# A gated recurrence with a cosine-gated two-layer block on one core: the second group's second layer as seven half-block products, and a read-back moved behind the first turned keys

## The chip, the cores and the metric

The kernel runs on one core of one Trainium2 chip. The core has a matrix engine (TensorE, PE in the profile, with its weight loads shown as PEld), a vector engine (VectorE, DVE), a scalar engine (ScalarE, ACT), GpSimd (POOL) and a queue engine (SyncE, SP) that issues most of the DMA transfers. ACT and POOL issue some transfers too (ACTq, POOLq). The metric is the device time of one run in microseconds, and the measure of a kernel is the median of its runs.

## The reference

There are 4 batches, 8 heads, 768 steps and 48 channels per head. The first part is a recurrence with a complex gate, and the second part is a layer pair on its output.

```python
mag = sqrt(a_re*a_re + a_im*a_im);  scale = minimum(mag, 0.999) / (mag + 1e-6)
for t in range(768):                       # per batch and head; S is 48 x 48, complex
    S = (a_re + i*a_im)[t] * scale[t] * S + outer(k[t], v[t])      # k, v are real
    y[t] = q[t] @ real(S)
x = y as (3072 tokens, 384)
h = x @ w_in                               # 384 x 2048
out = (h * cos(h)) @ w_out                 # 2048 x 384
```

## The kernel before, in words

The 768 steps of a batch are cut into chunks of 128, which gives 24 chunks in all. Two chunks make a group, so there are 12 groups, numbered from 0. Groups 0 and 1 are written out by hand, with their order on each engine fixed by the order of the text. From group 2 on, a loop over `n` places closures on a line from 0 to 1 with a function `weave`: each list of steps has a stretch of that line, and the steps are called in order of their places. A scheduling layer then gives each engine its own order. Every engine works through its own order, and a row that waits holds up all rows behind it on that engine.

One group passes through these steps, whose tile names are those of the profile:

- **Powers.** `log_steps` makes the logarithm of the gate (`lg`, `mag`, `rs`, `tan`), `p_powers` sums it over the steps of a chunk on PE (`lgs`) and makes `P` and `Q` by two exponentials each, `even_steps` rounds them, and `row_out` and `row_back` write the last row of `P` to memory (`row`) and read it back turned (`end`). `p_end` then scales `end`, which `state_next` needs. From group 2 on, `lg` and the angle are split into a high and a low part (`hi`, `lo`) before PE sums them (`lgs`, `phs`).
- **Keys.** `p_apply`, `g_phase` and `g_trig` make `ks` and `qs`, the queries and keys with the gates' powers and angles in them. Groups 0 and 1 turn them on PE (`turn`, tile `tp`) and ACT copies them out (`kT`, `qT`). From group 2 on, DVE transposes blocks (`tr`) and three transfers bring them into place (`moved`, `kT`, `qT`).
- **Chunk.** `f_scores` multiplies queries and keys (`sc`) and DVE masks them (`atm`); `state_sums` and `state_next` carry the state (`sp`, `state`); `f_out` makes the output (`yp`), ACT copies it (`yT`), and two transfers, one behind the other, turn it into the layers' input (`x<-yT`, then `xT<-x`).
- **First layer.** `mm1` multiplies (`hp`, 48 products of 128 x 256 per group), ACT takes the cosine (`gate`) and a sum of squares for a range check (`junk`), and DVE multiplies (`gate<-hp,gate`). There are eight `gate` tiles of 128 x 512, each with two blocks of 128 channels for the group's 256 tokens.
- **Second layer.** Groups 0 and 1 use `mm2`: for each of the two chunks, 16 products of 128 x 384 into one tile `op`, four at a time, which ACT then copies out. Groups 2 to 11 use seven products of half blocks, as in Strassen's method: `mixed` makes sums and differences of the gate's half blocks on DVE (four rows of 128 x 256 for each of four values of `p`, tiles `s` and `gate<-gate`), `quarters` and `last_quarter` make those of `w_out` once for all groups (12 rows `t_s`, `t_a` of 128 x 384 and 4 rows `w_out<-w_out`), and `seventh` runs one product: 8 matmuls of 128 x 192 in two parts of four. Products 0, 3, 5 and 6 add up in one tile (`sum`), the other three go to `op`.

The constant that decides is `PLAIN = 2`: groups below it use `mm2`. PE runs one 32-bit matmul of the text as two rows, so 16 matmuls show as 32 rows. Many rows carry the line of a helper: L687 is `matmul`, and L676 and L707 are the helpers through which all DVE rows and most ACT rows pass, so the tile names tell the steps apart.

Four places of the text matter for the change. In group 0, after the angles, the text has

```python
    row_back(0, 0, G, scalar)
    busy(10)
    g_stack(0, 0, 1)
    ...
    turn(0, 0)
    lows(0, 1)
    piece(0)
    f_scores(0, 0)
```

`row_back` with `scalar` issues its two transfers from ACT's queue, `busy` is idle work for PE, `lows` is an ACT step of the conversion of `w_in` and `w_out` from 64-bit numbers, and `piece` is a DVE step of it. The other three places are the load of group 1 (`load(1, ("re", "im", "k", "q", "v"))`, on SP), the text around group 1's first half of `mm2` (`upper = second(1, 0)`), and the `weave` of `n = 2`, in which group 1's second layer, group 2's chunks and group 3's powers lie side by side.

Of the kernel before, what the change touches and what calls it, by code (L numbers as in the profile page):

```python
# [11 lines left out]
F32 = mybir.dt.float32  # L12
# [7 lines left out]
ALU = mybir.AluOpType  # L20
# [467 lines left out]
def fast_path(ctx, tc, q, k, v, a_re, a_im, moe_w_in, moe_w_out, out, least, odd, wide,  # L488
# [7 lines left out]
    nc = tc.nc  # L496
    B, H, S, D = q.shape
    DM, DF = moe_w_in.shape
    C = 128
    NCH = S // C  # L500
    G = 2
    N = B * NCH
    NG = N // G
# [5 lines left out]
    NJ = DF // C  # L509
# [13 lines left out]
    pm = ctx.enter_context(tc.tile_pool(name="pm", bufs=3, space=PSUM))  # L523
# [10 lines left out]
    late = {}  # L534
# [8 lines left out]
    def behind(ins, other):  # L543
        tc.add_manual_dep(ins.ins, other.ins.name, mybir.DependencyInfo(
            mybir.DependencyClass.NoSync, mybir.DependencyReason.DATA))
# [15 lines left out]
    Y = [dict() for _ in range(N)]  # L561
# [5 lines left out]
    def load(g, names, i=None, put=nc.sync.dma_start):  # L567
        for name in names:
            ap = {"re": a_re, "im": a_im, "q": q, "k": k, "v": v}[name]
            if name not in X[g]:  # L570
                X[g][name] = ld.tile([C, G, H, D], F32, tag=name, name=name,
                                     bufs=2 if name == "v" else 1)
            b, c = divmod(g * G + (i or 0), NCH)
            one, n = i or 0, G if i is None else 1
            steps = ap[b].rearrange("h (c p) d -> p c h d", p=C)[:, ds(c, n)]
            tile_ = X[g][name][:, ds(one, n)]
            parts = [(0, C, 0)]
            if name in ("re", "im") and g >= PEG:

                parts = [(0, C - 16, 1), (C - 16, C - 1, 1)]  # L580
                put(out=tile_[C - 1:C], in_=steps[0:1])
            for i_ in range(n):
                for lo, hi, by in parts:
                    put(out=tile_[lo:hi, i_], in_=steps[lo + by:hi + by, i_])  # L584
# [99 lines left out]
    vector, scalar = Ordered(nc.vector, "vector"), Ordered(nc.scalar, "scalar")  # L684

    def matmul(out, **kw):
        chain(nc.tensor.matmul(out, **kw), "tensor")  # L687
# [27 lines left out]
    def spans(g):  # L715

        return [(i, 1) for i in range(G)] if g == 0 else [(0, G)]
# [120 lines left out]
    def row_back(g, i, n, queue):  # L838
        row = X[g]["row"][ds(i * DM, n * DM)]
        end = X[g]["end"][:, ds(i * H, n * H)]  # L840
        for a in range(2):
            queue.dma_start(out=end[ds(a * D, D)], in_=row.rearrange("(x d) -> d x", d=D))

    def p_even(g, i, n):
        for _ in even_steps(g, i, n):
            pass
# [254 lines left out]

    def mm2(g, i, j0, nj):
        if j0 == 0:
            Y[g * G + i]["op"] = pm.tile([C, DM], F32, tag="acc" if g == i else "m", name="op",
                                         bufs=1 if g == i else 2)
        ps = Y[g * G + i]["op"]
        for j in range(j0, j0 + nj):
            matmul(ps, lhsT=X[g]["gate"][j // 2][:, j % 2, ts(i, C)], rhs=w_out[:, j],
                   start=(j == 0), stop=(j == NJ - 1))
        if j0 + nj == NJ:  # L1110
            ot = msb.tile([C, DM], F32, tag="ot", name="ot")
            scalar.mul(out=ot, in_=ps, mul=1.0 / (in_scale * out_scale))
            nc.sync.dma_start(out=out[ts(g * G + i, C), :], in_=ot)
# [1 line left out]

    PLAIN, HJ, E2 = 2, NJ // 2, DM // 2
    b11, b12, b21, b22 = (w_out[:, ds(r * HJ, HJ), ds(c * E2, E2)]
                          for r in range(2) for c in range(2))  # L1120
    right = {"a11": b11, "a12": b21, "s3": b12, "s4": b22}
# [1 line left out]
    def quarters():  # L1123

        for name in "s1", "s2", "a22":
            right[name] = stage["pool"].tile([C, HJ, E2], F32, name="t_" + name)
        t1, t2, t4 = (right[name] for name in ("s1", "s2", "a22"))
        for j in range(0, HJ, 2):
            for t, a, b in (t1, b12, b11), (t2, b22, t1), (t4, b21, t2):
                vector.tensor_tensor(out=t[:, ds(j, 2)], in0=a[:, ds(j, 2)],  # L1130
                                     in1=b[:, ds(j, 2)], op=ALU.subtract)

    def last_quarter():

        for j in range(0, HJ, 2):
            yield lambda j=j: vector.tensor_tensor(
                out=b12[:, ds(j, 2)], in0=b22[:, ds(j, 2)], in1=b12[:, ds(j, 2)],
                op=ALU.subtract)
# [64 lines left out]
    def products(g, lo, hi):  # L1203
        if g < PLAIN:
            return []
        return [lambda p=p, part=part: seventh(g, p, part)
                for p in (0, 1, 3, 2, 5, 4, 6)[lo:hi] for part in range(2)]

    def mixes(g, lo, hi):
        return [lambda p=p: mixed(g, p) for p in range(lo, hi)] if g >= PLAIN else []  # L1210

    def weave(*parts):

        items = []
        for p, (part, lo, hi) in enumerate(parts):
            part = list(part)
            items += [(lo + (hi - lo) * (i + 0.5) / len(part), p, t)
                      for i, t in enumerate(part)]
        for _, _, t in sorted(items, key=lambda x: x[:2]):
            t()  # L1220
# [4 lines left out]
    def keys(g):  # L1225

        if not 0 <= g < NG:
            return
        for i, n in spans(g):
            yield lambda i=i, n=n: g_trig(g, i, n)  # L1230
            yield lambda i=i, n=n: (g_stack(g, i, n), p_end(g, i, n))
            for name in "kT", "qT":
                if g >= PEG:
                    yield lambda i=i, n=n, name=name: f_transpose(g, i, n, name)
# [4 lines left out]
    def powers(g):  # L1239
        return [lambda i=i: p_powers(g, i) for i in range(G)]  # L1240

    def prods(g):
        if not 0 <= g < NG:
            return
        if g not in (1, 2):
            yield from powers(g)
            yield lambda: g_angle(g, 0, G)
        yield lambda: (g_carry(g), g_split(g))
        yield lambda: (p_even(g, 0, G), p_apply(g, 0, G))

    def logs(g):
        yield from each(g_log, g)
        if 0 <= g and g + 1 < NG:
            yield lambda: load(g + 1, ("re", "im"))

    def phases(g):
        return [lambda i=i: g_phase(g, i) for i in range(G)] if 0 <= g < NG else []

    def chunks(g):
        for n in range(g * G, g * G + G):  # L1260
            for hh in range(2):
                yield lambda n=n, hh=hh: f_scores(n, hh)
            yield lambda n=n: f_state(n)
            yield lambda n=n: f_out(n)
        yield lambda: (f_x(g), f_xt(g))
        if g + 2 < NG:
            yield lambda: load(g + 2, ("k", "q", "v"))

    def first(g):
        order = range(NJ // 2) if g < PLAIN else (0, 4, 1, 5, 2, 6, 3, 7)  # L1270
        return [lambda jp=jp: mm1(g, jp) for jp in order]

    def second(g, i):
        return [lambda j0=j0: mm2(g, i, j0, 4) for j0 in range(0, NJ, 4)] if g < PLAIN else []

    def wait_for(tile):

        chain(nc.gpsimd.tensor_copy(out=after, in_=tile), "gpsimd")
# [14 lines left out]
    turns = [constant(sums_np[0] * np.float32(1.0 / math.pi), "turns", pool=stage["pool"])]  # L1293
    last = constant(last_np, "last", pool=stage["pool"])
    ident = constant(np.eye(C, dtype=np.float32), "ident", pool=stage["pool"])
    load(1, ("re", "im", "k", "q", "v"))
    ones = constant(sums_np[1], "sums_turned", nc.sync, stage["pool"])
    exact = consts.tile([C, C], F32R, name="exact")
    alls = consts.tile([C, C], F32R, name="alls")
# [26 lines left out]
    p_apply(0, 0, 1)  # L1326
    g_phase(0, 1)
    g_trig(0, 1, 1)
    row_back(0, 0, G, scalar)
    busy(10)  # L1330
    g_stack(0, 0, 1)
    p_apply(0, 1, 1)
# [12 lines left out]
    def lows(*ks):  # L1345
        for k in ks:
            pieces[k][1]()
# [14 lines left out]
    def turn(g, i):  # L1362
        for name in "kT", "qT":
            for hh in range(2):
                f_turn(g, i, name, hh)

    turn(0, 0)
    lows(0, 1)
    piece(0)
    f_scores(0, 0)  # L1370
# [180 lines left out]
    piece(15)  # L1551
    X[3]["steps"] = log_steps(3, 0, G)
    next(X[3]["steps"])
    upper = second(1, 0)
    for t in upper[:2]:
        t()
    sums(1, 6, 8)
    pair(12, 2)
# [3 lines left out]
        mm1_gate(1, jp)  # L1562
    room.close()
    stage.update(pool=ctx.enter_context(tc.tile_pool(name="late", bufs=1)), bufs=1)
    quarters()
    for n in range(2, NG):
        weave((mixes(n - 1, 2, 4), 0.0, 0.12), (logs(n + 1), 0.0, 0.02), (chunks(n), 0.0, 0.36),
              (upper[2:] if n == 2 else [], 0.0, 0.2), (products(n - 1, 0, 2 + (n < NG - 1)), 0.0, 0.36),
              (prods(n + 1), 0.25, 0.27), (second(n - 1, 1), 0.36, 0.5),
              (products(n - 1, 2 + (n < NG - 1), 7), 0.4, 0.56),  # L1570
              (phases(n + 1), *((0.472, 0.476) if n == PLAIN else (0.516, 0.524))),
              (keys(n + 1), *((0.5, 0.62) if n == PLAIN else (0.53, 0.64))),
              (last_quarter() if n == PLAIN else [], 0.9, 1.0), (first(n), 0.56, 1.0),
              (mixes(n, 0, 2), 0.9, 1.0), (guarded(n - 1, per) if n > 3 else [], 0.1, 0.9))
    checked = verdict(late)

# [96 lines left out]
```

## Time and profile before

| | |
|---|---|
| median of 3 runs | 657.82 us (657.73 to 659.49) |
| the profiled execution | 657.8 us, of which the profile spans 656.0 us |
| granted clock of TensorE, mean | 0.998 |
| PE busy | 641.3 us, 98% of the span, 4075 rows |
| PEld busy | 575.7 us, 88% |
| DVE busy | 492.4 us, 75%, 799 rows |
| ACT busy | 392.5 us, 60%, 726 rows |
| chain that ended last | PE 86%, DMA 6%, SP's queue 2%, DVE 2%, ACT 2% |

A row of the timeline has its start in the span, its duration (of all merged rows where it ends in xN), the engine, the line, the operation, the tiles as written from read, the shapes, and in square brackets how long the engine stood idle before it and what ended that. The duration of a row runs to its end; where rows of an engine follow each other without a wait, the distance from start to start is shorter than that, since they overlap.

### The profile page before, as it was taken

What the parts mean: (1) busy time and instruction counts of PE and PEld (TensorE: products, weight loads), DVE (VectorE), ACT (ScalarE), POOL (GpSimd) and SP (SyncE); (2) the same over time, 40 slices, a digit from 0 to 9 for tenths busy, and PEclk for the clock granted to TensorE, in tenths of its full rate; (3) what the DMA queues carried; (4) which work ended last, traced back from release to release, by engine and by line L of the source; (5) the groups of instructions that cost most, each with busy time, mean ns of one, the idle gap of its engine ahead of it and who ended that gap; (6) DMA issues with size and microseconds to landing.
All of it is one profiled execution on the core that took longest, in us unless ns stands there. A gap on an engine that the chain in (4) does not pass through costs nothing.

```text
span 656.0 us, 10759 instructions
## 1 busy us (share of the span) xinstructions
PE 641.3 (98%) x4075; PEld 575.7 (88%) x4075; DVE 492.4 (75%) x799; ACT 392.5 (60%) x726; POOL 32.0 (5%) x53
## 2 busy tenths in 40 slices
PE   8899999999999999999999999999999999999996
PEld 5688867777999899899899899899899999999996
DVE  6899989878687688786787777876877878862251
ACT  7788687293583594494585485485476476433330
POOL 4010100000000010010010010000000000000000
PEclk9999999999999999999999999999999999999999
DMA  9969664727626757737838736836936853364001
GB/s 239 224 187 219 196 189 102 190 60 181 145 49 151 186 135 157 193 98 167 217 78 182 206 92 160 207 95 133 245 104 133 224 127 94 112 135 119 25 1 31
DMA packets 232920, 94.90 MB, mean 145 GB/s; under 512 B 208701, under 2 KB 221246, under 8 KB 232858
## 3 DMA queue, kind: packets, MB, share of 16 engines
q1 hardware_dynamic: 225320, 68.51, 45.9%
q0 software_dynamic: 5824, 25.50, 11.9%
q8 instruction: 34, 0.56, 0.4%
q10 hardware_dynamic: 1714, 0.11, 0.2%
q14 instruction: 28, 0.23, 0.1%
HBM read 69.28 MB, written 24.81 MB: 143 GB/s over the span
## 4 chain that ended last, share of the span: by engine, by line
PE 86%; DMA 6%; SPq 2%; DVE 2%; ACT 2%; issue 1%; ACTq 0%; DVEq 0%
PE hp L687 34%; PE op L687 16%; PE sum L687 15%; PE sc L687 6%; PE yp L687 6%; PE sp L687 4%; DMA v<-in_v_dram 2%; PE phs L687 2%; SPq L584 1%; DMA xT<-x 1%; PE lgs L687 1%; DMA qT<-moved 1%; DMA x<-yT 1%; PE yr L687 1%; SPq L936 1%
## 5 line engine op out<-in xcount | busy, mean ns | idle before, releaser
L687 PE MATMUL hp<-xT,w_in 128*128 128x256 f32 (+1 forms) x1176 | 252.7, 376 | 1.0 <-DMA xT<-x 1.0
L687 PEld LDWEIGHTS hp<-xT,w_in 128*128 128x128 f32 x1176 | 219.9, 190 | 31.5 <-DMA xT<-x 0.9
L707 ACT ACTIVATE gate<-hp,half_pi_b 128x512 f32<-128x512 f32 x96 | 66.0, 687 | 120.2 <-PE hp L687 120.2
L676 DVE TENSOR_TENSOR gate<-hp,gate 128x512 f32<-128x512 f32 x96 | 65.7, 685 | 47.2 <-ACT junk L676 47.1
L687 PE MATMUL op<-w_out,gate 128*128 128x192 f32 (+1 forms) x448 | 100.7, 375 | 0.0
L687 PEld LDWEIGHTS op<-w_out,gate 128*128 128x128 f32 x448 | 76.0, 190 | 16.8 <-issue 2.0
L676 ACT ACTIVATE junk<-hp 128x512 bf16<-128x512 f32 x96 | 56.6, 590 | 0.0
L687 PE MATMUL sum<-t_s,s 128*128 128x192 f32 x320 | 56.3, 329 | 0.0
L687 PEld LDWEIGHTS sum<-t_s,s 128*128 128x128 f32 x320 | 52.1, 190 | 1.5 <-issue 1.5
L676 DVE TENSOR_TENSOR atm<-sc,causal 128x512 f32<-128x512 f32 x48 | 32.9, 688 | 25.7 <-PE sc L687 25.6
L687 PEld LDWEIGHTS sc<-qT,kT 96*128 96x128 f32 x384 | 47.2, 192 | 5.4 <-ACT qT L676 2.5
L687 PE MATMUL sc<-qT,kT 96*128 96x128 f32 x384 | 49.2, 277 | 2.5 <-ACT qT L676 2.3
L676 ACT ACTIVATE ot<-sum 128x192 f32<-128x192 f32 x40 | 12.8, 322 | 52.8 <-PE sum L687 52.6
L676 DVE SCALAR_TENSOR_TENSOR ot<-op,ot 128x192 f32<-128x192 f32 x41 | 13.6, 353 | 39.5 <-PE op L687 37.9
L687 PE MATMUL yp<-atm,v 128*48 128x128 f32 x352 | 33.6, 277 | 0.9 <-ACT Q L707 0.6
L703 ACT ACT_TABLE_LOAD x24 | 30.8, 1283 | 1.1 <-PEq L1657 0.7
L687 PE MATMUL yp<-qT,state 96*48 96x128 f32 x304 | 29.7, 272 | 0.0
L687 PE MATMUL sum<-w_out,gate 128*128 128x192 f32 x160 | 29.7, 330 | 0.0
L687 PE MATMUL sp<-v,ks 128*96 128x48 f32 x320 | 29.7, 246 | 0.0
L687 PEld LDWEIGHTS sp<-v,ks 128*96 128x96 f32 x320 | 29.6, 165 | 0.0
L676 ACT COPY yT<-yp 48x512 f32<-48x512 f32 x44 | 25.2, 573 | 7.4 <-PE yp L687 6.9
L676 ACT CAST tan<-phs 128x384 int32<-128x384 f32 x24 | 11.4, 482 | 29.4 <-PE phs L687 29.4
(145 smaller groups left out, 985.7 us busy)
## 6 DMA issues: line engine op xcount, KB each, us to landing
moved<-tr SPq DMA_DIRECT2D x20, 768.0 KB
raw<-in_moe_w_in_dram POOLq DMA_DIRECT2D x16, 768.0 KB, 5.3
raw<-in_moe_w_out_dram POOLq DMA_DIRECT2D x16, 768.0 KB, 4.9
kT<-moved SPq DMA_DIRECT2D x40, 192.0 KB
qT<-moved SPq DMA_DIRECT2D x10, 768.0 KB
k<-in_k_dram SPq DMA_DIRECT2D x24, 192.0 KB
q<-in_q_dram SPq DMA_DIRECT2D x24, 192.0 KB
v<-in_v_dram SPq DMA_DIRECT2D x24, 192.0 KB
```

What stands on the lines that cost most here:

```text
L584: put(out=tile_[lo:hi, i_], in_=steps[lo + by:hi + by, i_])
L676: ins = getattr(self.engine, op)(**kw)
L687: chain(nc.tensor.matmul(out, **kw), "tensor")
L703: chain(nc.scalar.preload_act_table_set(table))
L707: chain(nc.scalar.activation(func=func, **kw))
L936: nc.sync.dma_start(out=X[g][name][:, ds(i * H, n * H), q4], in_=moved[q4])
```

## The change

Group 1 joins the groups whose second layer is seven products (`PLAIN = 1`). Its first product is placed where the first half of `mm2` stood, and the others in the `weave` of `n = 2`. With it, all sixteen DVE rows of group 1's `mixed` come into that stage; `quarters` becomes a list of steps that is woven in there, and `last_quarter` moves from the end of that stage to its front. `mm2`, now used by group 0 alone, takes both its tiles from the two buffers "m" and none from "acc", which `sum` needs. In the start, `row_back` of group 0 moves behind `turn(0, 0)`, and the load of group 1's values `v` moves behind the loads of its gates, keys and queries. The scheduling layer had issued those two `v` loads right behind group 0's.

```diff
     def mm2(g, i, j0, nj):
         if j0 == 0:
-            Y[g * G + i]["op"] = pm.tile([C, DM], F32, tag="acc" if g == i else "m", name="op",
-                                         bufs=1 if g == i else 2)
+            Y[g * G + i]["op"] = pm.tile([C, DM], F32, tag="m", name="op", bufs=2)
...
-    PLAIN, HJ, E2 = 2, NJ // 2, DM // 2
+    PLAIN, HJ, E2 = 1, NJ // 2, DM // 2
...
         for j in range(0, HJ, 2):
             for t, a, b in (t1, b12, b11), (t2, b22, t1), (t4, b21, t2):
-                vector.tensor_tensor(out=t[:, ds(j, 2)], in0=a[:, ds(j, 2)],
-                                     in1=b[:, ds(j, 2)], op=ALU.subtract)
+                yield lambda t=t, a=a, b=b, j=j: vector.tensor_tensor(
+                    out=t[:, ds(j, 2)], in0=a[:, ds(j, 2)], in1=b[:, ds(j, 2)], op=ALU.subtract)
...
-    def second(g, i):
-        return [lambda j0=j0: mm2(g, i, j0, 4) for j0 in range(0, NJ, 4)] if g < PLAIN else []
...
-    load(1, ("re", "im", "k", "q", "v"))
+    load(1, ("re", "im", "k", "q"), put=lambda **kw: late.update(load=nc.sync.dma_start(**kw)))
+    load(1, ("v",), put=lambda **kw: behind(nc.sync.dma_start(**kw), late["load"]))
...
     g_trig(0, 1, 1)
-    row_back(0, 0, G, scalar)
     busy(10)
...
     turn(0, 0)
+    row_back(0, 0, G, scalar)
     lows(0, 1)
...
-    upper = second(1, 0)
-    for t in upper[:2]:
+    for t in products(1, 0, 1):
         t()
...
-    quarters()
     for n in range(2, NG):
-        weave((mixes(n - 1, 2, 4), 0.0, 0.12), (logs(n + 1), 0.0, 0.02), (chunks(n), 0.0, 0.36),
-              (upper[2:] if n == 2 else [], 0.0, 0.2), (products(n - 1, 0, 2 + (n < NG - 1)), 0.0, 0.36),
-              (prods(n + 1), 0.25, 0.27), (second(n - 1, 1), 0.36, 0.5),
-              (products(n - 1, 2 + (n < NG - 1), 7), 0.4, 0.56),
-              (phases(n + 1), *((0.472, 0.476) if n == PLAIN else (0.516, 0.524))),
-              (keys(n + 1), *((0.5, 0.62) if n == PLAIN else (0.53, 0.64))),
-              (last_quarter() if n == PLAIN else [], 0.9, 1.0), (first(n), 0.56, 1.0),
+        early, cut_ = n == 2, 2 + (n < NG - 1)
+        weave((mixes(n - 1, 0 if early else 2, 4), 0.0, 0.24 if early else 0.12),
+              (logs(n + 1), 0.0, 0.02), (chunks(n), 0.0, 0.36),
+              (quarters() if early else [], 0.01, 0.2), (last_quarter() if early else [], 0.3, 0.36),
+              (products(n - 1, int(early), cut_), 0.12 * early, 0.36),
+              (prods(n + 1), 0.25, 0.27), (products(n - 1, cut_, 7), 0.4, 0.56),
+              (phases(n + 1), 0.516, 0.524), (keys(n + 1), 0.53, 0.64), (first(n), 0.56, 1.0),
               (mixes(n, 0, 2), 0.9, 1.0), (guarded(n - 1, per) if n > 3 else [], 0.1, 0.9))
```

## The prediction

> **What bounds the kernel now.** The page first: PE is busy 98% of the span and carries 86% of the chain that ended last, so a microsecond that reaches PE's order in the middle reaches the end. But a share over the whole span does not say who sets the pace in the two stretches that the change touches, so I read their timelines. The start, first ACT's queue, then who waited:
>
> ```profile
> 22.93 1.02 ACTq L676 DMA_DIRECT2D end<-row  x2
> 24.00 1.07 ACT L676 COPY kT<-tp 96x512 f32<-96x512 f32 x2 [3.01 <-DMA v<-in_v_dram]
> 25.60 2.05 PE L687 MATMUL sc<-qT,kT 96*128 96x128 f32 x16 [2.28 <-ACT qT L676]
> 26.80 0.69 DVE L676 TENSOR_TENSOR atm<-sc,causal 128x512 f32<-128x512 f32 x1 [1.33 <-PE sc L687]
> ...
> 30.04 0.86 ACT L749 ACTIVATE lg<-re 128x768 f32<-128x768 f32 x1
> 31.67 0.96 DVE L676 TENSOR_TENSOR lg<-lg,tan 128x768 f32<-128x768 f32 x1
> 33.75 0.16 DVE L676 TENSOR_SCALAR end<-end 96x16 f32<-96x16 f32 x1
> ```
>
> ACT stands 3.01 us before it can copy keys that PE had turned from 21.30 on: its two `end` issues wait for older transfers, and the chain names the last `v` load (10.88, 12.75 us in flight). PE loses 2.28 us and DVE 1.33 us to that.
>
> From here to 122 us DVE is the engine without slack: the view of waits for that stretch has six entries, 3.7 us in 100. The middle, group 2's stage:
>
> ```profile
> 121.59 1.02 DVE L676 TENSOR_TENSOR t_s<-w_out 128x384 f32<-128x384 f32 x2
> ...
> 129.52 0.69 DVE L676 TENSOR_TENSOR atm<-sc,causal 128x512 f32<-128x512 f32 x1 [2.23 <-PE sc L687]
> ...
> 146.69 0.95 DVE L676 SCALAR_TENSOR_TENSOR lg<-mag,lg 128x768 f32<-128x768 f32 x1
> 147.71 0.24 SPq L835 DMA_DIRECT2D row<-lg  x1
> 148.04 1.51 SPq L1048 DMA_DIRECT2D x<-yT  x2
> 149.30 1.96 DVE L676 TENSOR_TENSOR w_out<-w_out 128x384 f32<-128x384 f32 x4
> ...
> 156.39 7.82 PE L687 MATMUL hp<-xT,w_in 128*128 128x256 f32 x35 [0.33 <-DMA xT<-x]
> ```
>
> Between 121.59 and 146.69 DVE idles in six places, 5.8 us in all (2.23, 0.46, 0.84, 0.62, 1.04, 0.62). The SP queue sends `row` when DVE's last `lg` is done and only then the `x` transfers behind it; `hp` of group 2 starts 8.35 us after the `x` issue. So two orders end in that `hp`: PE's products and DVE's way to `lg`.
>
> **Part 1, the start.** The move takes the `end` issues out from ahead of four copies. PE's `tp` rows start at 21.30 and 22.24, the first half of the keys is done at about 21.92. ACT is free from 20.98, so four copies (spacing 0.48) run from 21.95 to 23.95, against 24.00 to 26.04. `sc` starts at 23.5 and not at 25.60, and DVE's first mask follows its row of 24.91 without a wait. The two issues then stand on ACT between the last copy and the two `raw` rows of `lows`; they cost 0.34 + 0.31 us of issue if nothing holds them. `raw` ends near 26.6 (27.82 before), the next copies start 1.5 earlier (28.13 had waited 0.31 for PE), and `lg<-re` comes at 28.5. DVE's own order, with 1.33 and 0.20 of waiting gone, would bring 31.67 to 30.1; ACT allows the same. Gain: 1.5 us, and as DVE stays full until 122 us it is kept. No trace row shows what holds the moved issues: they now wait for `row` and for group 1's first `im` load, which takes the queue place of the `v` load that landed by 22.93. Bounds: 2.1 (ACT's whole shift) to 0. Holding `v` moves two loads of 192 KB on SP's queue behind `q`; group 1 uses them at 66 us, and its gates come forward. Nothing else waits for them, and I cost it at nothing.
>
> **Part 2, PE's products.** `mm2` of group 1 is 2 x 16 products in 64 rows of 384 columns; the chain has 16 such rows in 5.16 us, 0.3225 each, 20.64 us. Seven products are 56, 112 rows of 192; the chain has 16 in 2.60, 0.1625 each, 18.20. PE has 2.44 us less to do.
>
> One rule speaks against it. The Trainium skill, "TensorE: Matmul & The Clock Gate", section "Back-to-back issue gap", gives a sustained 81 ns at 128 columns and 131 ns at 512, because weight loads set part of the spacing. By a straight line between them (an estimate from that page) 192 columns cost 89 and 384 cost 115, and the change would add some 7 us where the rows take away 2.44. The rows halve with the columns, so I use the rows.
>
> **Part 3, DVE's work before `lg`.** By the order of the changed kernel's instructions, these rows now stand on DVE between 121.59 and the last `lg`: sixteen `mixed` rows, 0.34 apart (164.87 to 166.35 has four in 1.48, with one dependence), 5.44; the four `last_quarter` rows that stood behind it, 1.96; one eviction, 0.27; and one `Q<-k` row that stood behind `lg`, 0.87. Together 8.5. The twelve `quarters` rows were there already.
>
> Another rule makes this dearer: "VectorE: DVE Perf Modes", in its section on the errata, has (N+151)/0.96 ns for an fp32 add and a latency exposed at each instruction. At N = 256 that is 424 ns, an estimate that agrees with the 425 ns of these rows' durations; by it sixteen rows would be 6.8 and the sum below 1.4 worse. The starts are 0.34 apart, since the rows overlap, and I take the starts.
>
> Walk DVE's order from 121.59. Up to the first mask: 12 x 0.47 + 8 x 0.34 + 2 x 0.49 = 9.34, so 130.9 (129.5 before). Then four masks and two `gate` products at 0.60, the state at 2 x 0.47, eight more mixed rows, three wide rows at 0.87, one narrow at 0.47 and `lo<-lg,hi` itself at 0.95 end at 142.2. The rest brings `lg` to start at 148.9 to 149.1, 2.2 to 2.4 later: 8.5 more work less the idle 5.8, which is used up, with dependences of about 0.1 each between neighbours.
>
> Who waits: PE does `sum` (8 products, 2.60 for 5.16), `hp` and group 0's last `op`, and wants `sc` at 125.9 (128.42 less 2.56). `qT`'s issue of 120.84 must have landed; the DMA share falls from 1.06 to 0.13 at 126, so about 126.2. Then `sp` to 129.4, but `yp` needs the mask of 131.6: PE stands 2.3 us. It stands again ahead of `lgs`, until `lo` at 142.2: four us. So PE's 2.44 us are lost in new waits. From 142.3 PE has three `lgs` rows (0.5), `yp` (1.9), four products (64 rows, 10.4), `phs` (1.2 to 1.4), one more product (2.6): `hp` at 159.0. By the transfers, `x` 2.3 later gives 158.7. PE's is later: 159.0 against 156.39, a loss of 2.6.
>
> ACT gets a wait as well: its second copy of group 0's `op` now waits until the first one's output has landed, since `sum`'s tiles hold the other buffer. Queued behind it are two cosines, a table load and the `lg` rows. No row shows that landing; between `x<-yT`'s 2.8 (in the chain at 454.73) and `qT`'s 5.4 (120.84 to 126.2) after an issue at 125.2, it is 128.0 to 130.6. Up to 129 the rows behind it are still in time for DVE; at 130.6 DVE loses 1.1. I take nothing, since `x<-yT` is the nearer row in size and place. Group 0's tiles "m" cost nothing: the second needs `gate` 7, done at 82.16, when PE comes to it at 82.55; with that cover gone it would be tenths.
>
> **Sum.** The later stages keep their order, and their `sc` stays at the end of 20.7 us of `hp`, so the shift stays: 657.8 (the profiled execution, 656.0 of span and 1.8 around it; the median is 657.82) - 1.5 + 2.6 = 658.9 us. Bounds of the middle: +3.7 with ACT's 1.1, and -2.4 if DVE were no limit.
>
> **Rivals.** Slower: the two `end` reads land after DVE wants them. DVE's `p_end` would come to 32.2 and all its rows stand behind. They are issued near 24.0 to 24.6 in a stretch where the DMA engines are full until 30 (shares 1.01 to 1.32), where a `v` load took 12.75 us. Against it, they are 3 KB each, and before they had 9.8 us, now 7.6. From 33.1 on the kernel is over 0.3% slower; at 33.75 the gain is gone, 660.4; at 12.75 us of flight it is 664. Same side, smaller: ACT's late output, 660.0.
>
> Faster: DVE's added rows find their cover after all, because the order leaves PE enough other work. Then 1.5 and 2.44 both count: 653.9; with half of it, 656.4. For it: DVE is idle 5.8 us there, and 25% of the span. Against it: the added rows stand ahead of the masks, not in the idle places.
>
> **Chances.** What a measurement of this kernel can tell from no change is about 0.3%, 1.97 us, so 655.8 to 659.8 is "same". Forecast 0.58 (0.49 same, 0.08 slower, 0.01 faster: it spreads about a microsecond); slower rival with ACT's 0.22 (0.20 slower, 0.02 same); faster rival 0.20 (0.13 faster, 0.07 same). That makes 0.14, 0.58 and 0.28. The range 655.6 to 661.2 leaves out most of the full faster case and the far end of the slower one.
>
> **What would show it.** Right: `sc` of chunk 0 at 23.5, `lg<-lg,tan` of group 1 near 30.1, everything to 121 earlier by 1.5; then PE waiting for `atm` ahead of group 2's first `yp` by some 2 us and for `lo` ahead of `lgs` by some 4; `hp` of group 2 at 157.5 on the new axis. Wrong: ACT idle ahead of `raw` or DVE ahead of `end` near 32 (the slower rival), or no wait of PE at `lgs` (the faster one).

## The result, and the profile after

The changed kernel takes 663.64 us (median of 8 runs, 660.76 to 667.10), the kernel before, run beside it, 657.78. The medians differ by 5.9 us. The ratio, worked out over the runs of both kernels, is 1.0077, 95% interval 1.0057 to 1.0097, which is 5.1 us slower; the differences below go by such ratios. The median lies 2.4 us beyond the upper end of the range. The profiled execution took 663.11 us with a span of 661.2 and a mean granted clock of 0.993 (0.998 before).

The start, in the timeline of the changed kernel:

```profile
22.00 1.07 ACT L676 COPY kT<-tp 96x512 f32<-96x512 f32 x2 [1.00 <-PE tp L948]
23.44 0.93 ACTq L676 DMA_DIRECT2D end<-row  x2
23.60 2.05 PE L687 MATMUL sc<-qT,kT 96*128 96x128 f32 x16 [0.27 <-ACT qT L676]
...
28.14 0.86 ACT L749 ACTIVATE lg<-re 128x768 f32<-128x768 f32 x1
29.77 0.96 DVE L676 TENSOR_TENSOR lg<-lg,tan 128x768 f32<-128x768 f32 x1
...
31.84 0.16 DVE L676 TENSOR_SCALAR end<-end 96x16 f32<-96x16 f32 x1
```

The start did what it should, and a little more: `lg<-lg,tan` of group 1 is 1.90 us earlier (31.67 before), the same row of group 3 1.99 us (118.73 for 120.72), and DVE finds `end` landed. So whatever made the kernel 5.1 us slower cost 7 us after that. The middle, by engine, DVE and SP's queue first and then PE:

```profile
118.73 0.94 DVE L676 TENSOR_TENSOR lg<-lg,tan 128x768 f32<-128x768 f32 x1
...
128.83 1.27 DVE L676 TENSOR_TENSOR atm<-sc,causal 128x512 f32<-128x512 f32 x2
...
139.10 0.95 DVE L676 SCALAR_TENSOR_TENSOR lo<-lg,hi 128x768 fp32r<-128x768 f32 x1
...
147.29 0.95 DVE L676 SCALAR_TENSOR_TENSOR lg<-mag,lg 128x768 f32<-128x768 f32 x1
...
148.31 0.24 SPq L835 DMA_DIRECT2D row<-lg  x1
148.65 0.81 SPq L1048 DMA_DIRECT2D x<-yT  x2
```

```profile
125.83 2.02 PE L687 MATMUL sc<-qT,kT 96*128 96x128 f32 x16 [1.79 <-DMA qT<-moved]
...
129.56 0.43 PE L687 MATMUL yp<-atm,v 128*48 128x128 f32 x4 [0.39 <-DVE atm L676]
...
138.28 0.44 PE L687 MATMUL lgs<-hi,exact 128*128 128x384 f32 x1 [2.16 <-ACT hi L728]
140.10 0.69 PE L687 MATMUL lgs<-lo,exact 128*128 128x384 f32 x1 [1.38 <-DVE lo L676]
...
144.95 3.45 PE L687 MATMUL sum<-t_s,s 128*128 128x192 f32 x16
148.23 2.76 PE L687 MATMUL op<-t_a,gate 128*128 128x192 f32 x16
...
159.67 2.54 PE L687 MATMUL hp<-xT,w_in 128*128 128x256 f32 x11
```

PE stands where the prediction said it would, 2.2 us around the chunk's scores and 3.5 us ahead of `lgs`. What it did not say is in the rows after that: the first product takes 3.45 us, the second, with the same number of rows of the same size, 2.76. The windows' table has the reason in its column PEclk (the columns are the length of the window, busy us and rows of PE, PEld, DVE, ACT and POOL, the granted clock, the DMA share and GB/s):

```profile
138.00:140.00 2.00, 0.44 (x1) 0.19 (x1) 2.00 (x4) 0.23 (x1) 0.00 (x0) 0.83 0.64 119
140.00:146.00 6.00, 5.90 (x38) 5.07 (x39) 5.55 (x9) 4.70 (x8) 0.00 (x0) 0.50 0.46 89
146.00:148.00 2.00, 2.00 (x13) 2.00 (x13) 1.71 (x3) 0.97 (x2) 0.00 (x0) 0.96 0.08 15
```

In finer windows the clock falls to 0.50 at 139.33 and is whole again at 146.16. PE had gone idle at 136.1. From the `lgs` that ended the wait (140.10) PE ran 6.06 us at half speed. The theory to test: the stall was about as long as predicted, but it lowered the granted clock, and that took another 3 us. That is less than half of the 7; what the rest is, the experiments show in part.

### The profile page after: what moved, and what is told of

Its sections match the earlier page's. It is cut to its first block, busy times and chain, and to the rows that moved or that the text cites. A ratio compares the mean times of both kernels' runs of the same rounds, so it can differ in the third digit from the quotient of the medians.

```text
span 661.2 us, 10876 instructions
## 1 busy us (share of the span) xinstructions
PE 642.9 (97%) x4123; PEld 584.3 (88%) x4123; DVE 498.3 (75%) x819; ACT 393.0 (59%) x728; POOL 30.8 (5%) x53
## 4 chain that ended last, share of the span: by engine, by line
PE 78%; DVE 10%; ACT 5%; DMA 4%; issue 2%; SPq 1%; DVEq 0%
PE hp L687 33%; PE sum L687 15%; PE op L687 11%; PE yp L687 5%; PE sc L687 5%; PE sp L687 3%; PE phs L687 2%; DVE w_out L676 1%; DMA xT<-x 1%; PE lgs L687 1%; ACT rs L707 1%; ACT tan L707 1%; DVE mag L676 1%; DMA qT<-moved 1%; DMA im<-in_a_im_dram 1%
## 5 line engine op out<-in xcount | busy, mean ns | idle before, releaser
L687 PE MATMUL op<-w_out,gate 128*128 128x192 f32 (+1 forms) x416 | 84.8, 353 | 0.0
L687 PEld LDWEIGHTS op<-w_out,gate 128*128 128x128 f32 x416 | 69.2, 190 | 9.5 <-issue 1.9
L687 PE MATMUL sum<-t_s,s 128*128 128x192 f32 x352 | 62.5, 331 | 0.0
L687 PEld LDWEIGHTS sum<-t_s,s 128*128 128x128 f32 x352 | 57.9, 192 | 1.8 <-issue 1.8
L676 DVE SCALAR_TENSOR_TENSOR ot<-op,ot 128x192 f32<-128x192 f32 x45 | 15.0, 353 | 45.0 <-PE op L687 43.4
L687 PE MATMUL sum<-w_out,gate 128*128 128x192 f32 x176 | 32.4, 329 | 0.0
L687 PE MATMUL op<-t_a,gate 128*128 128x192 f32 x176 | 30.4, 326 | 0.0
```

Of the source, the lines that this page charges most:

```text
L676: ins = getattr(self.engine, op)(**kw)
```

## Experiments

Each run is compared with the kernel before on its own chip; `hp` stands for the start of group 2's `hp` (156.39 before, 159.67 after; the expectations say 159.84, from the chain's modelled ends).

### The two parts apart

`e1_start` is the kernel before with this alone:

```diff
-    load(1, ("re", "im", "k", "q", "v"))
+    load(1, ("re", "im", "k", "q"), put=lambda **kw: late.update(load=nc.sync.dma_start(**kw)))
+    load(1, ("v",), put=lambda **kw: behind(nc.sync.dma_start(**kw), late["load"]))
...
-    row_back(0, 0, G, scalar)
     busy(10)
...
     turn(0, 0)
+    row_back(0, 0, G, scalar)
```

> The kernel before with the start part alone: the ends of the first group's powers behind the first copies of turned keys, and v held behind q. Theory (the start's gain is kept by DVE's full order and is worth its whole shift of 2.0 us): hp of group 2 at 154.4 (156.39 before), 655.8 us in all. Rival (the gain is lost again in group 2's stage, where sc waits for qT and hp for x, whose transfers are not set by DVE alone): hp of group 2 at 156 or later, 657.5 to 658 us.

Measured: 656.69 us against 659.34, ratio 0.9963 (0.9944 to 0.9982), 2.4 us faster; `hp` at 154.32. The theory holds: the start's whole shift reaches the end.

`e2_middle` takes the same lines out of the changed kernel.

> The changed kernel without the start part: the second group's half products alone. Theory (the two parts add): everything to 121 us as in the kernel before, hp of group 2 some 5.4 us later than there, near 161.8, 665 us in all. Rival (the middle's loss comes from the earlier start meeting a transfer that did not move, qT or x): PE's waits for qT are shorter here and the total is 661 to 663 us.

Measured: ratio 1.0121 (1.0089 to 1.0153), 8.0 us slower. The parts add: -2.4 and +8.0 make 5.6, and both together measured 5.1. `hp` came at 164.04 and not 161.8, but this execution reached the stage 2.3 us late: in its start PE stood 2.34 us for the turned keys, and the clock was at 0.62 from 28 to 32. From the last `op` of group 0 to `hp` it needs 41.0 us, the changed kernel 40.95 (118.72 to 159.67).

### The clock held, with work that is thrown away

```diff
         ps = pa.tile([C, DM], F32, tag="a", name="lgs")
+        for _ in range(16 if g == 3 and i == 0 else 0):
+            matmul(ps[:, 0:2 * C], lhsT=w_in[:, 0, 0, 0:C], rhs=w_in[:, 0, 0],
+                   start=True, stop=True)
         summed_up(ps, g, i, "lg", upto[0])
```

> The changed kernel with sixteen products of 256 columns, 3.5 us by the hp rows, on PE ahead of group 3's lgs, where it stood idle; their result is overwritten. Theory (PE's idle time lowered the granted clock, and that cost 3.0 us of work from 140 to 146): PEclk 1.00 throughout 138 to 148, yp x32 in 1.9 us and not 3.6, hp of group 2 at 156.9 to 157.3, total 2.7 to 3.8 us below the changed kernel, near 660 us. Rival (the slow rows are due to something else in that stretch, DVE at full load or the bank that yp shares): yp stays near 3.6 and the total within 0.5 us of the changed kernel's, or above it since the added rows stand on PE's order.

The dose was wrong: a product is two rows, so sixteen took 6.7 us and pushed `lgs` to 142.78. The reading is still good. The clock stayed at 1.00 and `yp` took 1.9 us again; with `lgs` from `lo` 3.04 us later than in the changed kernel, `hp` came 0.13 us later (159.80). The ratio is 1.0065 (1.0035 to 1.0095), not to be told from the changed kernel's. `e5_warm_half` is the same with eight.

> The changed kernel with eight products of 256 columns on PE ahead of group 3's lgs (each takes two rows, so the sixteen of the run before took 6.7 us and moved lgs from 138.28 to 142.78). Eight should take 3.4 us, from 136.1 to 139.5, where PE stands anyway until lo at 140.1. Theory (the clock cost 3.0 us of the middle): PEclk 1.00 from 130 to 150, yp x32 in 1.9 us, hp of group 2 at 157.0 (by PE 156.8, by x 157.0) and not 159.84, total 2.5 to 3 us below the changed kernel's, about 1.003 of the kernel before. Rival (x or phs is next, so the clock's 3.0 us were covered): hp of group 2 at 159 or later, ratio still near 1.008.

Its PE timeline, and its row of the windows' table:

```profile
136.21 3.62 PE L687 MATMUL lgs<-w_in 128*128 128x256 f32 x16
139.47 0.53 PE L687 MATMUL lgs<-hi,exact 128*128 128x384 f32 x1
140.36 0.44 PE L687 MATMUL lgs<-lo,exact 128*128 128x384 f32 x1 [0.36 <-DVE lo L676]
...
142.99 2.87 PE L687 MATMUL sum<-t_s,s 128*128 128x192 f32 x16
...
157.13 8.15 PE L687 MATMUL hp<-xT,w_in 128*128 128x256 f32 x37
```

```profile
140.00:146.00 6.00, 5.64 (x53) 5.20 (x54) 5.80 (x9) 5.11 (x9) 0.00 (x0) 1.00 0.35 66
```

In the same six microseconds PE does 53 rows where it had done 38. `lo` is no earlier (140.36 for 140.10), no wait behind it was touched, and `hp` is 2.54 us earlier: from that `lgs` to `hp` 16.77 us for 19.57. The ratio is 1.0011 (0.9993 to 1.0029), 4.3 us less than the changed kernel's. So 3.3 us of useless work on PE (136.21 to 139.47) take back five sixths of the loss. That the lowered clock cost 2.5 us up to `hp` is shown. The other 1.8 of the 4.3 come behind `hp`, and the theory does not cover them. Some of it may be further drops: three of the changed kernel's eight runs had a mean clock of 0.985 to 0.988, below the 0.993 of the profiled one, while ten of the twelve runs here had 0.998 or more.

### What holds lgs

```diff
-              (quarters() if early else [], 0.01, 0.2), (last_quarter() if early else [], 0.3, 0.36),
+              (quarters() if early else [], 0.01, 0.2), (last_quarter() if early else [], 0.42, 0.44),
...
-            yield lambda j=j: vector.tensor_tensor(
-                out=b12[:, ds(j, 2)], in0=b22[:, ds(j, 2)], in1=b12[:, ds(j, 2)],
-                op=ALU.subtract)
+            yield lambda j=j: behind(vector.tensor_tensor(
+                out=b12[:, ds(j, 2)], in0=b22[:, ds(j, 2)], in1=b12[:, ds(j, 2)],
+                op=ALU.subtract), X[3]["powers"])
```

Here `X[3]["powers"]` is the row that writes `lg` in group 3's powers.

> The changed kernel with its four last_quarter rows (1.9 us on DVE) held behind the powers' last row lg, ahead of which they stood. Theory (DVE's order sets the stall, and the stall the clock): first mask 0.95 us earlier, lo near 138.1, lg near 145.4, PE's idle ahead of lgs 3.5 us before and about 1.6 now; if that is too short to lower the clock, hp of group 2 near 155 and the total near 658.5 us; if the clock falls all the same, 661.5. Rival (PE's own order or the x transfers set the end): lg earlier by 1.9 but hp of group 2 within 0.5 us of 159.8 and the total near 663.

A miss: ratio 1.0084 (1.0051 to 1.0116). The first masks came 0.82 us earlier (128.01), since only two of the four rows had stood ahead of them and of `lo`. `lo` gained 0.54, since an eviction of 0.27 now stands ahead of it. DVE has no idle time between the first mask and `lo` in this run, and none in the changed kernel, so its order is what sets `lo`. The clock fell all the same, and `hp` was at 159.09. The first `lgs` row waited for `hi`, which did not move; ACT's timeline of this run shows why:

```profile
126.54 0.49 ACT L676 ACTIVATE ot<-op 128x384 f32<-128x384 f32 x1 [3.21 <-DMA out_dram<-ot]
...
131.54 0.58 ACT L676 COPY yT<-yp 48x512 f32<-48x512 f32 x1
...
133.63 0.58 ACT L676 COPY yT<-yp 48x512 f32<-48x512 f32 x1
...
137.37 0.83 ACT L728 ACTIVATE hi<-lg 128x768 fp32r<-128x768 f32 x1
```

ACT has no gap from 126.54 to `hi`, and the `yT` copies now stand ahead of it. In the kernel before they stood behind it:

```profile
138.45 0.83 ACT L728 ACTIVATE hi<-lg 128x768 fp32r<-128x768 f32 x1
...
139.19 1.16 ACT L676 COPY yT<-yp 48x512 f32<-48x512 f32 x2
```

`e6_orders` adds the following to this run, and `e7_act_only` adds it to the changed kernel alone (`X[3]["half"]` is `hi` of group 3):

```diff
-            scalar.copy(out=X[g]["yT"][half, :, i], in_=ps[half])
+            put = scalar.copy(out=X[g]["yT"][half, :, i], in_=ps[half])
+            if n == 4:
+                behind(put, X[3]["half"])
```

> The run with the late last_quarter, and ACT's two first yT copies of group 2 held behind hi, which they had delayed on ACT from 131.6 on. Theory (ACT's order held hi at 138.2 and so lo, which is why the late last_quarter gained only 0.5 us there): hi done at 136.3, lgs from hi at 136.4, from lo at 138.4, PE's idle ahead of them 2.2 us in all; hp of group 2 at 158.0 if the clock falls all the same and at 155 if not; ratio 1.005 or 1.001. Rival (hi is held by something else): lgs from hi stays at 138.2.

> The changed kernel with the two yT copies behind hi and last_quarter where it was. In the built order three mixed rows follow behind lo with that, and one eviction comes ahead of it. Theory: lgs from hi at 136.4, lo done 0.7 us earlier, lgs from lo at 139.3; PE's idle time is nearly the same in sum (3.1 for 3.5 us) and the clock falls again; hp of group 2 near 159.0, ratio 1.006 to 1.008. Rival (ACT's order alone is the cause of the stall): lo follows hi at once and the ratio falls to 1.003 or below.

Measured: ratios 1.0022 (1.0005 to 1.0039) and 1.0031 (1.0015 to 1.0048). `e7_act_only` is well below what was expected of it, near its rival. With `hi` no longer behind `yp` the built order also puts three `mixed` rows behind `lo`; in its profile the two gaps ahead of `lgs` are 1.55 and 1.26 us, the clock stays up there, and from group 0's last `op` to `hp` it needs 35.81 us, since on PE this execution reached the stage 4 us late and found `qT` landed. On DVE it was only 2.4 us late (`lg<-lg,tan` at 121.16), and from that row `lo` comes 0.72 us sooner than in the changed kernel: three rows of 0.34 fewer ahead of it and an eviction of 0.27 more. In `e6_orders` `lgs` from `hi` came at 137.83 and not 136.4: it reached the stage 1.8 us late, the first output landed at 127.1, and ACT had waited 2.01 us for it; the clock fell for a part (0.79 in the mean of 138 to 146), and `hp` came at 157.30. So two orders hold `lgs`: ACT's holds `hi`, and DVE's holds `lo`. The edit to ACT's order, with the three rows that it moved on DVE, was worth more than half of what `e5_warm_half` gave; how much of that is ACT's alone, and how much the clock that stayed up, these two runs do not separate.

### The orders rebuilt, and POOL

`e8_rebuilt` moves more: gates 6 and 7 of group 1 ahead of group 0's last outputs, `quarters` ahead of the `weave`, group 3's log rows behind the masks, `mixed` 2 and 3 behind `lo`. Of its diff against `e6_orders`:

```diff
     sums(1, 6, 8)
     pair(12, 2)
+    for jp in 6, 7:
+        mm1_gate(1, jp)
     pair(14, 2)
...
+    for t in quarters():
+        t()
     Ordered.by_hand, Ordered.mark = (), dict(tail)
-    for jp in 6, 7:
-        mm1_gate(1, jp)
...
+            if g == 1 and p > 1:
+                behind(ins, X[3]["lower"])
```

The last two lines stand in `mixed`, and `X[3]["lower"]` is group 3's `lo`.

> Both parts of the change with the orders of the three engines rebuilt around it: gates 6 and 7 ahead of group 0's last outputs on ACT and DVE, quarters ahead of the weave, group 3's log rows behind the first masks, yT copies behind hi, mixed 2 and 3 behind lo, last_quarter behind lg. From the rows: hi at 134, masks of chunk 4 at 126.9 to 128.2, lo at 136.6, PE's idle ahead of lgs 1.3 us, clock 1.00, lg at 144, x at 145, hp of group 2 at 153.3; against 154.32 in the run with the start part alone that is 1.0 us less, ratio 0.995 (0.9963 there). Rival (the half products give nothing that the start alone doesn't, since DVE's work ahead of lg or the transfers of x set that hp): hp at 154.3 or later, ratio 0.996 to 1.000.

A miss, by 7 us at `hp`: ratio 1.0074 (1.0052 to 1.0097), `hp` at 160.62. Gates 6 and 7 write the buffers that group 0's last products still read: ACT stood 7.41 us for PE's `op` and DVE, whose order now had the gates in front, 3.10 and 1.89 us; the first `yp` waited 4.16 us for its mask. That cover was never there, and the run is no test of the theory for the middle. The clock fell here too, from 132.32 on, while PE stood for that mask.

`e9_pool` is `e7_act_only`, and `e10_start_pool` is `e1_start`, with the sixteen subtractions on POOL; in `quarters`, and alike in `last_quarter`:

```diff
-                yield lambda t=t, a=a, b=b, j=j: vector.tensor_tensor(
+                yield lambda t=t, a=a, b=b, j=j: nc.gpsimd.tensor_tensor(
```

> Both parts of the change, the two yT copies behind hi, and the sixteen subtractions of quarters and last_quarter on POOL, which does nothing from 86 us on: 7.6 us less on DVE ahead of lg. No row shows POOL at this work; up to 1.6 us for each row it is done in time for the product that reads it at 138. Theory (DVE's work ahead of lg was the price of the half products): masks of chunk 4 at 126.8 as soon as sc is there, hi at 136.3, lo at 137.2, PE's idle ahead of lgs under 1.5 us and the clock 1.00, hp of group 2 at 153.9, ratio 0.9957, as good as the start part alone or a little better. Rival (POOL's rows are too slow, or slow DVE's down beside them): PE waits for t_s in products after the second yp, hp of group 2 at 156 or later, ratio 1.000 or more.

> The start part alone with the same sixteen subtractions on POOL. Here they stood where DVE had idle time behind them (2.22 us ahead of the first mask in the run of the start part). Theory (in this order PE and ACT set hp of group 2, not DVE): hp of group 2 at 154.3 as in that run, the ratio 0.996 within 0.002. Rival (DVE's earlier work helps there too): hp at 153 or earlier, ratio 0.994.

`e9_pool` is slower than all others but `e2_middle`: 1.0104 (1.0083 to 1.0125), `hp` at 162.49. POOL's rows were in time: no product waited for them, and they were 0.97 us apart where DVE had no `mixed` rows. But of the `mixed` rows on DVE beside them, the later ones, 0.34 apart elsewhere, were 1.14 apart, as POOL's and DVE's lines show. The first eight (119.70 to 122.46) kept their 0.34; there it was POOL that was slow:

```profile
119.22 5.05 POOL L1132 TENSOR_TENSOR t_s<-w_out 128x384 f32<-128x384 f32 x2 [32.95 <-DVE w_out L676]
...
129.96 2.66 POOL L1132 TENSOR_TENSOR t_s<-w_out,t_s 128x384 f32<-128x384 f32 x2
132.58 2.33 POOL L1132 TENSOR_TENSOR t_a<-w_out,t_s 128x384 f32<-128x384 f32 x2
134.87 6.47 POOL L1138 TENSOR_TENSOR w_out<-w_out 128x384 f32<-128x384 f32 x4
```

```profile
132.83 1.22 DVE L676 TENSOR_TENSOR s<-s,gate 128x256 f32<-128x256 f32 x1
133.97 1.22 DVE L676 TENSOR_TENSOR gate<-gate 128x256 f32<-128x256 f32 x1
135.11 1.21 DVE L676 TENSOR_TENSOR s<-gate,s 128x256 f32<-128x256 f32 x1
136.25 0.94 DVE L676 SCALAR_TENSOR_TENSOR mag<-re,mag 128x768 f32<-128x768 f32 x1
```

The work left DVE and DVE became slower; `lo` ended at 143.0 and PE stood 4.17 and 1.98 us ahead of `lgs`. `e10_start_pool`, without `mixed` rows there, lost nothing and won nothing: 0.9958 (0.9942 to 0.9974), `hp` at 154.46.

### Both mended at once

`e11_orders_warm` is `e6_orders` with five thrown-away products, `e12_mixes_late` has three, and `mixed` 2 and 3 behind `lo` as in `e8_rebuilt`.

```diff
+        for _ in range(5 if g == 3 and i == 0 else 0):      # 3 in e12_mixes_late
+            matmul(ps[:, 0:2 * C], lhsT=w_in[:, 0, 0, 0:C], rhs=w_in[:, 0, 0],
+                   start=True, stop=True)
```

> The run with last_quarter behind lg and the yT copies behind hi, and five products of 256 columns (ten rows, 2.15 us) on PE ahead of lgs. Theory (what is left of the changed kernel's loss is the clock plus DVE's and ACT's order ahead of lo, and they add): PEclk 1.00 in 130 to 150, lgs from lo at 138.4 when the stage begins as in the changed kernel, hp of group 2 at 155.3, ratio 0.998 to 0.999. Rival (the clock and the order are one gain, taken twice): ratio 1.001 as with the eight products alone.

> The same with three products instead of five and the mixed rows of products 2 and 3 held behind lo, so that DVE has 2.4 us less ahead of it. Theory (lo then follows hi, which ACT has done at 136.4): lo at 137.2, PE's idle under a microsecond, hp of group 2 at 154.1, within 0.3 us of the run with the start part alone (154.32), and 0.6 us lost in group 3's stage as in the other runs with the half products: ratio 0.997, not below that of the start alone. Rival (the half products' 2.44 us of PE come through once DVE is out of the way): hp of group 2 below 153.5, ratio 0.994.

Measured: 1.0001 (0.9979 to 1.0022) and 1.0010 (0.9985 to 1.0036). In the profile of `e12_mixes_late` the clock stays at 1.00 and `hp` comes at 155.16, a microsecond later than expected since `lo` came at 138.3. Its runs fall in two groups. The six with a granted clock of 0.998 or more took 656.7 to 658.3 us, the six with 0.990 to 0.993 took 660.3 to 664.4. The profile of `e11_orders_warm` (clock 0.994) shows where such a drop can come: not ahead of `lgs`, which the added products cover, but at the wait for `qT`.

```profile
126.00 2.40 PE L687 MATMUL sc<-qT,kT 96*128 96x128 f32 x16 [1.95 <-DMA qT<-moved]
```

```profile
124.00:126.00 2.00, 0.05 (x1) 0.03 (x1) 2.00 (x6) 0.00 (x0) 0.00 (x0) 1.00 0.41 134
126.00:128.00 2.00, 2.00 (x16) 2.00 (x17) 2.00 (x6) 1.73 (x5) 0.00 (x0) 0.87 0.19 66
128.00:130.00 2.00, 2.00 (x14) 2.00 (x14) 1.85 (x4) 1.98 (x4) 0.00 (x0) 0.50 0.14 45
```

One gap of 1.95 us was enough there, for 6.83 us at half clock (127.49 to 134.32 in finer windows); `hp` came at 157.95. By the medians the theory of two gains is not told from its rival: 1.0001 and 1.0010 stand beside the 1.0011 of `e5_warm_half`, and the intervals overlap. Between two profiles without a drop, `e5_warm_half` and `e12_mixes_late`, `hp` comes 1.97 us earlier (157.13, 155.16). So the order can be a second gain, but the first stands open at a second place. Of the half products' 2.44 us on PE nothing was left in any run: the runs without a drop lie around 657.1 (the five of `e11_orders_warm` with a clock of 0.998 or more) and 657.3 (the six of `e12_mixes_late`), no better than `e1_start` with 656.69. That one beats both kernels, and is the version to keep.

## Why the prediction was wrong, point by point

**The start** was right in mechanism and too small: 1.90 to 1.99 us and not 1.5, within its bound of 2.1. The two `end` issues left ACT idle for 0.38 us ahead of `raw` (24.42), and not for 0.65. The slower rival did not come about; `end` had landed at 31.84.

**DVE's walk** was right. On the new axis (2.0 earlier) it puts the first mask at 128.9, the end of `lo` at 140.2 and `lg` 2.2 to 2.4 later; measured 128.83, 140.05 and 2.59 (147.29 against 144.70). Its own sum for the last, 8.5 of work less 5.8 of idle time, is 2.7 and not 2.2 to 2.4, and was the better of the two. The starts of 0.34 held. So did the rows of PE: a product of 16 rows takes 2.60 from start to start (148.23 to 150.83), where the rule on the gap between products would have had the change cost PE time. The 7 us that the prediction gives for that rule are not what its two figures make as they stand (112 rows at 89 less 64 at 115 ns are 2.6 us); one gets there only by raising the 20.64 us in their proportion.

**PE's waits** were right in sum, and only in part in name. `qT` landed at 125.8, 6.6 us after its issue at 119.16 and not 5.4, so PE stood 1.79 us there and 0.39 for the mask, for 2.3 all at the mask. Ahead of `lgs` it stood 3.54, for "four". Of that, 2.16 ended with ACT's `hi`, which the prediction did not name, because it costed ACT's order at nothing; but the stall as a whole ends with `lo`, which it did name.

**ACT's wait for the first output** was there (2.48 us):

```profile
125.76 0.49 ACT L676 ACTIVATE ot<-op 128x384 f32<-128x384 f32 x1 [2.48 <-DMA out_dram<-ot]
...
131.58 0.58 ACT L676 COPY yT<-yp 48x512 f32<-48x512 f32 x1 [0.76 <-PE yp L687]
...
137.40 0.83 ACT L728 ACTIVATE hi<-lg 128x768 fp32r<-128x768 f32 x1
```

In the changed kernel ACT then stood 0.76 us for `yp`, so the wait was not what decided; with the copies moved (`e6_orders`) ACT has no such pause from that output to `hi`. The nothing was right for a reason not given.

**The step that failed** is the next one: "From 142.3 PE has three `lgs` rows (0.5), `yp` (1.9), four products (64 rows, 10.4)". It priced PE's rows after a stall at what they take in a kernel whose PE hardly ever stalls, and put the clock at nothing. From the `lgs` that ends the stall to `hp` it has 16.7 us; `e5_warm_half`, with the clock at 1.00, took 16.77, the changed kernel 19.57. With the clock held, `e5_warm_half` puts `hp` at 157.13; the prediction said 157.5. With the clock falling, it is 159.67. That is 2.5 us of the 4.7 by which the forecast of 658.9 missed (4.0 by the ratio), and the run with the clock held measured 658.63 us (ratio 1.0011). That it lies so near the 658.9 is partly luck: the start gave half a microsecond more than forecast, and group 3's stage took 0.6 us (51.0 for 50.4) that the prediction had at nothing.

**"The shift stays"** failed as well, by 1.4 us against the kernel before: the changed kernel is 3.28 us later at group 2's `hp` and 4.68 at group 3's. Against `e5_warm_half` the difference goes from 2.54 us at group 2's `hp` to 3.33 at group 3's, back to 2.73 at groups 7 and 8, to 3.86 at group 9's, where the changed kernel's `hp` waits 0.96 us for `xT`, and to 4.3 at the end of the span. In group 3's stage the changed kernel's `sc` waits 0.82 us for `qT` and its `hp` 0.27 for `xT`.

**Still open** is what sets these later waits. From group 2's `hp` to group 3's the kernels without the half products need 50.3 to 50.4 us, those with them 50.3 (`e3_warm`) to 52.2 (`e9_pool`), 51.8 in the changed kernel. Two outputs of group 1 are now sent ahead of group 3's `moved` transfers, where one was; that alone is not the cause, since `e3_warm` sends two as well. What goes along with the loss is the time that SP's queue spends on issuing group 3's four `kT` transfers: 4.8 to 5.1 us in the four kernels that need 50.3 or 50.4, 5.2 and 5.8 in the two that need 51.0 (`e5_warm_half`, `e4_quarter_late`), 6.3 to 6.8 in the eight that need 51.3 to 52.2. Why it takes longer there was not tried.

## What to carry to other kernels

A wait that is put on TensorE is priced twice: by its length, and by the work behind it at the lower clock that it may bring, here 2.5 to 3 us for a stall of 3.5. So before an edit that trades PE's work for a wait of about two microseconds or more, ask what else could stand in the gap; where nothing can, useless products that fit into it cost next to nothing (`lgs` came 0.26 us later in `e5_warm_half`) and hold the clock. And look past the name of the wait: here the longer part of the stall (2.16 us) ended with a row of ACT, which had only been reordered, but the row that ended the whole was held by DVE, which had been filled up.

## What the runs showed of the hardware

The granted clock knows two values in these traces, 1.00 and 0.50, and the drops in the middle of a run lasted 3.41 us (the first of `e2_middle`, `e6_orders`, `e7_act_only`), 6.83 (the changed kernel, the second of `e2_middle`, `e4_quarter_late`, `e8_rebuilt`, `e11_orders_warm`) or 10.24 (`e9_pool`). The Trainium skill, "TensorE: Matmul & The Clock Gate", section "What's actually happening", has these two steps and a free-running window of 3413 ns; these are one, two and three such windows, and the trace agrees. Drops of one trace also start whole windows apart: 116.05 us in `e2_middle` (27.63 and 143.68), 34 windows, and 518.83 us in the changed kernel, 152 windows, from 139.33 to the drop after its last product (658.16). The page's section "HAM oscillation" asks for no idle gap over about 3.4 us. Here shorter ones sufficed: drops followed gaps of 1.95 (`e11_orders_warm`), 2.08 (`e7_act_only`, for `xT` of group 1 at 86) and 2.34 us (`e2_middle`), while gaps of 1.85 (`e6_orders`), 2.22 (`e12_mixes_late`), 2.28 (the start of the kernel before) and 2.36 (`e9_pool`, for `qT`) passed in the profiled executions.

Laid on that grid of 3.41 us, the traces show what told them apart. In the window ahead of each of the nine drops PE was busy, by its rows, for 8 to 43% of the time (19% in the changed kernel, 0.64 us between 135.92 and 139.33; 43% in `e11_orders_warm`). In every other window at full clock, from 16 to 645 us in all 14 traces, it was busy for 46% or more. So what counted here is PE's idle time within one window, more than some 1.9 us of it (an estimate from these shares), in one gap or several: a gap of two microseconds lowers the clock when it lies within a window, and passes when an edge divides it. What brings the clock back is less plain: windows at half clock with 20 to 77% busy did not, and of the full ones one did not either (`e11_orders_warm`). That the edges fall elsewhere in each execution may be why the runs of one kernel spread over as much as 7.6 us (`e12_mixes_late`); that is not shown. It fits that `e1_start`, whose `sc` in the start waits 0.27 us and not 2.28, had a clock of 0.997 or more in all its 12 runs, and that its gain was 2.4 us where its profile shows a shift of 2.0, though the interval of that gain (1.2 to 3.7) holds both.

DVE's `TENSOR_TENSOR` with both inputs in SBUF went from 0.34 to 1.14 us a row beside POOL's later subtractions, and POOL's first two rows took 5.05 us beside `mixed` rows that kept their 0.34, for 2.37 without such rows (`e10_start_pool`). The Trainium skill, "SBUF — State Buffer", section "Who interferes with whom", says that such a DVE instruction contends with a GpSimd instruction that reads SBUF, and for `TENSOR_TENSOR` the traces agree. The `SCALAR_TENSOR_TENSOR` at 136.25 has two such inputs too, and kept its 0.94 us; why is open.
